# Keeping the last four V heads across the turn, with attention and layernorm in columns and wo read in long rows

## The chip, the cores and the metric

The kernel runs on one core of one Trainium2 chip. The time is the device time of the whole program in microseconds (us). Before the change its median is 1688.55 us over 3 runs, from 1687.66 to 1689.11. The core's engines are TensorE (PE, with its weight loads PEld), VectorE (DVE), ScalarE (ACT), GpSimd (POOL) and SyncE (SP). Each takes its instructions in its own order. SP issues the large transfers, which all go into one DMA queue; POOL issues a few small ones.

## What is computed

One decode step of a transformer block, and its backward pass. With B = 4 sequences, one query position, D = 512, H = 32 heads of Dh = 128, a cache of Sk = 4096 positions and F = 1792:

```
q  = layernorm(x) @ wq                        # B x H x Dh
p  = softmax(q . K / sqrt(Dh))                # per (b, h), over 4096 positions
O  = p . V                                    # per (b, h), 128 values
h  = x + concat(O) @ wo                       # B x 512
h2 = h + (silu(n @ w1) * (n @ w3)) @ w2       # n = layernorm(h)
```

The outputs are h2 and the gradients of x, of the K cache and the V cache (128 MiB each), of wq, wo, w1, w3 and w2, for a given gradient of h2. The caches are bf16; there are NH = 128 pairs (b, h), here called heads and numbered s, with b = s mod 4. The K or V of one head is 1 MiB. K and V are read once for the forward pass, V again for the backward pass (dP = dO . V), and dK and dV are written.

## The kernel before

**The arena.** Nearly all large data live in one on-chip arena of 23 slots of 8,320 bytes per partition; a slot holds the K or V of a head, a product, a page of wo, or half of w1 or w3 (`Slot`). `manual_schedule` keeps the program order as written: the order of the Python text is the order of each engine's queue, and a transfer is issued when its slot is free and SP has come to it.

**Forward.** Groups of two heads run through a loop. For each head s, K gives the scores and the softmax weights P; DVE multiplies K by P (`PK_mul`, L457, 2.29 us each); PE multiplies V by PK and P in 32 matmuls of 130 columns (`M_mm`, L472, 2.03 us), which gives a matrix M that the backward pass uses for dq, and in its last column the head's output O; `M_end` sums P*K (L482), and ACT copies M out (L486). `O_cols` (L502) picks the O column of 16 heads out of M. V's slot is given back after each head. Toward the end, `weights` also loads the four pages of wo (L586) and the four halves of w1 and w3 (L580).

**The middle.** After head 125's M comes a stretch that isn't a loop. `attn_page` (L517) multiplies O by one page of wo (8 heads) into rows of 512, interleaved with the products of heads 126 and 127; DVE adds the pages to x. Then layernorm of h in rows: transposes of h, statistics, the mean and inverse deviation spread to all partitions by a matmul, `hhatT` (L873). Then gate and up (`gu_ps`, L880, 56 matmuls of four columns each), with w1 and w3 transposed in place on PE between them (`pt_w`, L601; copied back by ACT and DVE, L254 and L256) because the backward pass needs them the other way. silu and its derivative follow on DVE, then `dn_ps` (L911), the gradient at the layernorm's output, with 112 matmuls. The layernorm backward gives `dhT` (L950). wo is also transposed in place, two heads at a time (`woT`, L610).

**Turn and backward.** `rep_ps` (L958) spreads dO of the first heads over all partitions; `grad_V` (outer product on DVE, L813; store L824) makes dV of head 0 and head 1. `dO_columns` gives dO for 32 heads. V of the first heads is loaded a second time (`load_V2`, L840), nine of them before the first store. Each V is transposed in four groups on PE and ACT (`V_T`, L798 and L799), then `front(s)` (through POOL's `zd`, L1211) computes dP for the softmax backward. Groups 0 and 1 of head 0 are transposed during the layernorm backward, groups 2 and 3 after `dO_columns`. `front(0)` stands ahead of the third `grad_V`. From there on the loop over heads, later over pairs (L1400), loads V, makes dV and dK and stores them, with weight gradients as side work.

The heads are worked in the order s = 0 to 127 in both passes.

Of the kernel before, what the change touches and what calls it, by code (L numbers as in the profile page):

```python
# [15 lines left out]
G = 2  # L16
# [7 lines left out]
OLD = 9  # L24


@with_exitstack
def kernel(
# [58 lines left out]
    def bh_of(s):  # L87
        return s % B, s // B

# [72 lines left out]
    rows_t = pers.tile([32 + B, D], FP32, name="rows_t")  # L162
    xr, xhat = rows_t[0:B, :], rows_t[32:32 + B, :]
    nc.gpsimd.dma_start(out=xr, in_=x2)
    gr_s = Slot("gr")
# [7 lines left out]
    Ks, Vs, KTs, PKs = {}, {}, {}, {}  # L173

    def load_K(s):
        if s < NH:
            Ks[s] = Slot("Kn")
            nc.sync.dma_start(out=Ks[s].heads(), in_=cache_head(A_k_cache, s))
# [3 lines left out]
    def load_V(s):  # L182
        if s < NH and s >= nvl["n"]:
            nvl["n"] = s + 1
            Vs[s] = Slot("Vn")
            nc.sync.dma_start(out=Vs[s].heads(), in_=cache_head(A_v_cache, s))
# [16 lines left out]
    sel_f = fcon.tile([P, H], FP32, name="sel_f")  # L203
# [37 lines left out]
    hrows = xr  # L241
    kPT = pers.tile([P, NH], FP32, name="kPT")
# [83 lines left out]

    def M_of(s):
# [38 lines left out]
    def q_stationaries(gi):  # L366
        W = fw.tile([P, G, 4, 32], BF16, name="W", tag="W", bufs=1)
        for hl in range(G):
            s = gi * G + hl
# [69 lines left out]
    def sm_P(gi):  # L439
# [5 lines left out]
        for q in range(4):  # L445
            r_ = slice(32 * q, 32 * (q + 1))
            nc.scalar.copy(out=P_all[r_, gi * G:(gi + 1) * G, :].rearrange("p g (c jj) -> p g c jj", c=4),  # L447
                           in_=v[r_, 0:G, :, :, q])

    def PK_pairs(s):  # L450
        PKs[s] = Slot("PK")
        PK = PKs[s].t[:].rearrange("p (j c) -> p j c", c=PKW)
        nc.gpsimd.tensor_copy(out=PK[:, :, Dh:PKW], in_=P_all[:, s, :, None].to_broadcast([P, SJ, 2]))  # L453
# [20 lines left out]
    def M_end(s):  # L474
# [13 lines left out]
        Vs.pop(s).give()  # L488

    def kP_flush(s):  # L490
        ks = Slot("kP_sb")
        kP_sb = ks.f(4 * Dh).rearrange("p (c d) -> p c d", c=4)
        nc.scalar.copy(out=kP_sb, in_=hold["kP"][:])
        kt_ps = psM.tile([P, PKW], FP32, tag="M", name="kt_ps")
        for c in range(4):
            nc.tensor.matmul(kt_ps[:, 0:H], lhsT=kP_sb[:, c, :], rhs=sel_f[:], start=(c == 0), stop=(c == 3))
        nc.scalar.copy(out=kPT[:, s - 31:s + 1], in_=kt_ps[:, 0:H])
# [3 lines left out]
    def O_cols(s0, s1):  # L501
        nc.vector.tensor_copy(out=OT_f[:, s0:s1], in_=Ms[s0 // MC].f(MC * (Dh + 1)).rearrange("p (n c) -> p n c", c=Dh + 1)[  # L502
            :, s0 % MC:s0 % MC + s1 - s0, Dh])
        nc.vector.tensor_copy(out=OT_bf[:, s0:s1], in_=OT_f[:, s0:s1])
# [5 lines left out]
    def attn_page(pg):  # L510
        last = pg == H // 8 - 1
        if pg == 0 or last:
            hold["at"] = psT.tile([P, 512], FP32, tag="tps", name="al_ps") if last else psX.tile([P, 512], FP32, tag="x", name="at_ps")
        at_ps = hold["at"]
        for k in range(8):
            c = 0 if last else k % 2
# [1030 lines left out]
```

## Time and profile before

| what | value |
|---|---|
| median of 3 runs | 1688.55 us |
| span of the profiled execution | 1686.6 us |
| PE, DVE, ACT, POOL busy | 75%, 73%, 57%, 23% of the span |
| bytes moved | 707.21 MB, mean 419 GB/s |
| share of the large queue | 99.2% |
| V heads loaded singly, loads of two heads | 160, 48 |
| one product M (32 matmuls) | 2.03 us |
| one PK_mul or grad_V on DVE | 2.29 us |
| gate's first matmul | at 678.49 us |
| first dV store issued | at 699.11 us |

The profiled execution's own time is its span of 1686.6 us; the timed runs are about 2 us longer, which includes what lies around the span. A row of a timeline gives the start, the duration, the engine, the line, the operation, output and inputs, the number of instructions, and in brackets the engine's idle time before it and what ended that. Rows of PE can overlap with rows of its weight loads. The DMA share is the mean over 16 DMA engines.

### The profile page before, as it was taken

The numbers are of one execution on the slowest core, as the hardware profiler recorded it, in microseconds if no ns is written. First come the engines' busy times: TensorE is split into PE (matmuls) and PEld (weight loads), VectorE is DVE, ScalarE is ACT, GpSimd is POOL, SyncE is SP. The second block draws the span as 40 slices with busy tenths as digits, with TensorE's granted clock in tenths as the row PEclk, the third lists the DMA queues.
The fourth block names the chain that finished last, engine by engine and source line by source line (L and its number), as shares of the span: only waits on it lengthen the run. The fifth ranks groups of instructions, "written<-read, shape, count | busy, mean of one in ns | idle before, by whom it ended". The sixth has DMA issues, their size and how long they took to land.

```text
span 1686.6 us, 33967 instructions
## 1 busy us (share of the span) xinstructions
PE 1260.6 (75%) x14188; PEld 924.3 (55%) x14188; DVE 1233.9 (73%) x1198; ACT 960.9 (57%) x1492; POOL 379.6 (23%) x663
## 2 busy tenths in 40 slices
PE   5989888888888888878878666667766677776660
PEld 4777777677667766745555544544434444444440
DVE  5999899989998997667766476576565656555673
ACT  3455454445445454677666556666655676666650
POOL 1221222222232222234541131111120101011020
PEclk9999999999999999799899778777678676567775
DMA  9999999999999999999999999999999999999996
GB/s 400 424 424 424 425 423 425 424 424 421 418 423 411 424 411 397 398 410 426 425 426 428 429 429 429 431 430 429 429 430 430 429 429 431 430 429 431 430 429 259
DMA packets 80986, 707.21 MB, mean 419 GB/s; under 512 B 8748, under 2 KB 12984, under 8 KB 15296
## 3 DMA queue, kind: packets, MB, share of 16 engines
q1 hardware_dynamic: 80416, 704.94, 99.2%
q8 instruction: 112, 1.84, 0.4%
q14 instruction: 42, 0.34, 0.0%
q0 software_dynamic: 416, 0.10, 0.0%
HBM read 422.59 MB, written 282.34 MB: 418 GB/s over the span
## 4 chain that ended last, share of the span: by engine, by line
DMA 35%; DVE 7%; ACT 5%; PE 5%; issue 3%; DVEq 0%; SPq 0%; POOL 0%; ACTq 0%
DMA out_dram<-arena 34%; DVE arena L1400 7%; ACT arena L799 5%; PE pt_tps L798 1%; PE dq_ps L1007 1%; PE dP_ps L1245 1%; DMA arena<-in_A_v_cache_dram 1%; PE pt_wo L610 0%; DVEq L1542 0%; PE rep_ps L1186 0%; DVE dPr L1342 0%; ACT dPr L1221 0%; PE dOT_ps L773 0%; PE dPT_ps L1228 0%; PE c_ps L784 0%
## 5 line engine op out<-in xcount | busy, mean ns | idle before, releaser
L799 ACT COPY arena<-pt_tps 128x1024 bf16<-128x1024 bf16 x512 | 491.7, 1023 | 249.0 <-PE pt_tps L798 247.3
L798 PE MATMUL pt_tps<-ident_f,arena 128*128 128x128 f32 x2048 | 410.7, 356 | 202.9 <-DMA arena<-in_A_v_cache_dram 125.6
L798 PEld LDWEIGHTS pt_tps<-ident_f,arena 128*128 128x128 f32 x2048 | 304.1, 182 | 349.3 <-issue 191.6
L1400 DVE TENSOR_TENSOR arena<-arena 128x8192 bf16<-128x8192 bf16 x48 | 212.5, 4427 | 197.9 <-DMA out_dram<-arena 192.5
L457 DVE TENSOR_TENSOR arena<-arena 128x4096 bf16<-128x4096 bf16 x128 | 292.4, 2285 | 24.0 <-POOL arena L453 24.0
L472 PE MATMUL M_ps<-arena 128*128 128x130 bf16 x4096 | 286.9, 223 | 30.0 <-DMA arena<-in_A_v_cache_dram 29.2
L472 PEld LDWEIGHTS <-arena 128*128 128x128 bf16 x4096 | 254.6, 99 | 49.6 <-DMA arena<-in_A_v_cache_dram 42.5
L1400 DVE TENSOR_TENSOR arena<-dS,arena 128x8192 bf16<-128x8192 bf16 x48 | 212.3, 4424 | 67.6 <-DMA out_dram<-arena 67.6
L364 DVE STREAM_TRANSPOSE arena<-arena 128x512 f32<-128x512 f32 (+1 forms) x321 | 250.6, 797 | 0.0
L359 ACT COPY arena<-pt_tps 128x1024 bf16<-128x1024 bf16 x128 | 129.4, 1012 | 180.4 <-PE pt_tps L358 149.6
L1397 POOL COPY arena<-arena 128x128 bf16<-128x128 bf16 x48 | 43.7, 912 | 432.7 <-ACT arena L1374 200.0
L370 POOL TENSOR_TENSOR W<-qrep,wmask 128x128 bf16<-128x128 bf16 x128 | 120.8, 944 | 85.4 <-PE S_ps L390 70.6
L453 POOL COPY arena<-P_all 128x64 bf16<-128x64 bf16 x128 | 32.7, 256 | 412.5 <-ACT P_all L447 409.5
L1308 POOL COPY arena<-arena 64x4 bf16<-64x4 bf16 x96 | 68.8, 717 | 136.3 <-PE dP_ps L1328 108.6
L1328 PE MATMUL dP_ps<-arena 128*32 128x512 bf16 x768 | 84.4, 471 | 8.4 <-ACT arena L799 8.3
L813 DVE TENSOR_TENSOR arena<-dS,arena 128x4096 bf16<-128x4096 bf16 x32 | 73.1, 2291 | 21.8 <-DMA out_dram<-arena 21.5
L447 ACT COPY P_all<-pt_P 32x64 bf16<-32x64 bf16 x256 | 52.1, 203 | 54.1 <-PE pt_P L443 51.8
L358 PE MATMUL pt_tps<-ident_b,arena 128*128 128x128 bf16 x1024 | 80.8, 224 | 0.0
L482 PE MATMUL kP_ps<-arena,onesw 128*32 128x512 bf16 x1024 | 79.4, 387 | 0.0
L813 DVE TENSOR_TENSOR arena<-P,arena 128x4096 bf16<-128x4096 bf16 x29 | 66.3, 2291 | 17.7 <-DMA out_dram<-arena 17.5
L422 ACT ACTIVATE E<-S_ps,nm 128x256 f32<-128x256 f32 x64 | 30.4, 474 | 82.7 <-DVE nm L419 82.6
L991 PE MATMUL gps<-arena 4*128 4x512 bf16 x110 | 47.3, 452 | 39.0 <-ACT arena L985 39.0
(246 smaller groups left out, 1494.7 us busy)
## 6 DMA issues: line engine op xcount, KB each, us to landing
out_dram<-arena SPq DMA_DIRECT2D x96, 2048.0 KB, 27.4
arena<-in_A_v_cache_dram SPq DMA_DIRECT2D x160, 1024.0 KB, 15.6
arena<-in_A_k_cache_dram SPq DMA_DIRECT2D x128, 1024.0 KB, 15.4
arena<-in_A_v_cache_dram SPq DMA_DIRECT2D x48, 2048.0 KB, 31.7
out_dram<-arena SPq DMA_DIRECT2D x72, 1024.0 KB, 19.8
arena<-in_A_wq_dram SPq DMA_DIRECT2D x8, 1024.0 KB, 14.3
arena<-in_B_w_dram SPq DMA_DIRECT2D x8, 896.0 KB, 15.0
out_dram<-arena SPq DMA_DIRECT2D x6, 896.0 KB, 27.6
```

The source lines that it names most:

```text
L358: nc.tensor.transpose(pt[:, i, :], Kn[:, c * GW + i, :], ident_b[:])
L359: nc.scalar.copy(out=KT[:, c * GW:(c + 1) * GW, :], in_=pt[:])
L364: nc.vector.transpose(out=KT[:, c * w_:(c + n) * w_], in_=Kn[:, c * w_:(c + n) * w_])
L370: nc.gpsimd.tensor_tensor(out=W[:, hl], in0=qrep[:, :, s:s + 1].to_broadcast([P, 4, 32]), in1=wmask[:, hl, None, :].to_broadcast([P, 4, 32 ...
L457: nc.vector.tensor_tensor(out=PK[:, :, 0:Dh].rearrange("p j (r t) -> p j r t", t=2), in0=Ks[s].heads().rearrange("p j (r t) -> p j r t", t=2),
L472: nc.tensor.matmul(hold["M"][:], lhsT=Vn[:, j, :], rhs=PK[:, j, :], start=(j == 0), stop=(j == SJ - 1))
L482: nc.tensor.matmul(hold["kP"][32 * q:32 * (q + 1), :, :], lhsT=ones_window(w), rhs=PK[:, j0:j0 + 4, 0:Dh], start=(w == 0 and c == 0), stop ...
L798: nc.tensor.transpose(ptw[:, jj, :], w[:, 4 * g + jj, :], ident_f[:])
L799: nc.scalar.copy(out=v.rearrange("p (j d) -> p j d", d=Dh)[:, g * GW:(g + 1) * GW, :], in_=pt[:])
L813: nc.vector.tensor_tensor(out=dst.rearrange("p j (r t) -> p j r t", t=2), in0=col2[:, :, None, :].to_broadcast([P, SJ, Dh // 2, 2]), in1=r ...
L1328: nc.tensor.matmul(rows["acc"][32 * c:32 * (c + 1), :], lhsT=zt[t % B][:, k, ZP - m:ZP - m + 32], rhs=words_of(v, 2 * c + u, k), start=(pl ...
L1400: nc.vector.tensor_tensor(out=dst.rearrange("p (j r t) -> p j r t", r=Dh // 2, t=2), in0=col2[:, :, None, :].to_broadcast([P, 2 * SJ, Dh / ...
```

## The change

It has these parts.

- **The heads' order.** Forward step f works on head col(f) = (f + 4) mod 128, so the last four steps are heads 0 to 3, the first of the backward pass. Their V slots aren't given back but kept (`kept`), and the second loading of V starts at head 4. Four V loads of 1 MiB fall away.
- **wo in rows of 4096 bytes.** A page's element order in the arena is now head, then partition p, then four consecutive rows 4p to 4p+3 of wo, instead of one row per partition. `O_mix` rearranges O to fit, with 16 small matmuls against every fourth column of the identity and a DVE copy (`Omix`).
- **Attention as columns.** `attn_x` puts x into the accumulator `at_ps` [128, 4, 4], from x loaded once more in columns by four small POOL transfers at the start (`xcols`). `attn_heads` then multiplies wo by O with four columns at a time: 16 matmuls for one step of four heads. `attn_page` goes.
- **The tail's order.** Before M_mm of head 126 stand `O_cols`, `O_mix` and `attn_heads(1, 2)`; the DVE copies of `O_cols` come behind `PK_mul(127)`. The last `O_cols`, `O_mix` and `attn_heads` come behind the last product.
- **Layernorm as columns.** Two matmuls against ones (`col_sums`) give the sums over partitions; `hc`, `sq`, `rb` and `hhatT` are built from `hT_f`. The rows of h and of the normalised h are made later, during the backward pass.
- **Transposes.** `woT_unit` now turns four heads (16 transposes, two copies). A slot `w1T` takes the first half of w1 transposed, so that the half itself is given back earlier. The w1 and w3 transposes are spread differently: one unit during the layernorm, four and one of wo between gate and up, the rest interleaved with `dn`. One wo unit takes the place of V of head 0 in the shadow of the layernorm backward, and all four groups of V of head 0 come after `dO_columns`.
- **silu.** What depends on the gate alone is done between gate and up.
- One constant of the later side work (`S0`) goes from 21 to 23.

```diff
+    def col(f):
+        return (f + KEEP) % NH
...
-    rows_t = pers.tile([32 + B, D], FP32, name="rows_t")
-    xr, xhat = rows_t[0:B, :], rows_t[32:32 + B, :]
+    rows_t = pers.tile([P, D], FP32, name="rows_t")
+    xr, xhat, hhat = (rows_t[i:i + B, :] for i in (0, 32, 96))
     nc.gpsimd.dma_start(out=xr, in_=x2)
+    xcols = rows_t[64:64 + DC * B, 0:P]
+    for c in range(DC):
+        nc.gpsimd.dma_start(out=xcols[c * B:(c + 1) * B, :], in_=x2[:, c * P:(c + 1) * P])
...
-        Vs.pop(s).give()
+        if s < NH - KEEP:
+            Vs.pop(s).give()
+        else:
+            kept[col(s)] = Vs.pop(s)
...
     def wo_page(h):
         return mid_w["wo"][h // 8].b(8 * D).rearrange("p (h c n) -> p h c n", h=8, c=DC)
 
 
-    def attn_page(pg):
-        last = pg == H // 8 - 1
-        if pg == 0 or last:
-            hold["at"] = psT.tile([P, 512], FP32, tag="tps", name="al_ps") if last else psX.tile([P, 512], FP32, tag="x", name="at_ps")
-        at_ps = hold["at"]
-        for k in range(8):
-            c = 0 if last else k % 2
-            nc.tensor.matmul(at_ps[32 * c:32 * c + B, :], lhsT=OT_bf[:, (8 * pg + k) * B:(8 * pg + k + 1) * B],
-                             rhs=wo_page(8 * pg)[:, k].rearrange("p c n -> p (c n)"),
-                             start=(k == 0 if last else pg == 0 and k < 2), stop=(k == 7 if last else pg == H // 8 - 2 and k >= 6),
-                             tile_position=(0, 32 * c))
-        if pg >= H // 8 - 2:
-            for c in range(1 if last else 2):
-                nc.vector.tensor_tensor(out=hrows, in0=hrows, in1=at_ps[32 * c:32 * c + B, :], op=ALU.add)
+    def attn_x():
+        hold["at"] = psX.tile([P, DC, B], FP32, tag="x", name="at_ps")
+        r_ = slice(64, 64 + DC * B)
+        nc.tensor.matmul(hold["at"].rearrange("p c b -> p (c b)"), lhsT=xcols, rhs=ident_f[r_, r_], start=True, stop=False)
+
+    def O_mix(c0, c1):
+        ps = psT.tile([P, 4, H // 4, B], FP32, tag="tps", name="mix_ps")
+        ov = OT_bf.rearrange("p (c i b) -> p i c b", i=4, b=B)
+        for k in range(4):
+            for i in range(4):
+                nc.tensor.matmul(ps[32 * i:32 * (i + 1), k, c0:c1, :], lhsT=ident_b[:, k:P:4], rhs=ov[:, i, c0:c1, :],
+                                 start=True, stop=True, tile_position=(0, 32 * i))
+        nc.vector.tensor_copy(out=Omix[:, :, c0:c1, :], in_=ps[:, :, c0:c1, :])
+
+    def attn_heads(c0, c1, last=False):
+        for c in range(c0, c1):
+            wn = mid_w["wo"][c // 2].b(8 * D).rearrange("p (c k j) -> p c k j", c=2, k=4)[:, c % 2]
+            for k in range(4):
+                for jj in range(DC):
+                    nc.tensor.matmul(hold["at"][:, jj, :], lhsT=wn[:, k, jj * P:(jj + 1) * P], rhs=Omix[:, k, c, :],
+                                     start=False, stop=last and c == c1 - 1 and k == 3 and jj == DC - 1)
...
-        nc.sync.dma_start(out=sl.b(8 * D).rearrange("p (h j) -> p h j", h=8),
-                          in_=A_wo[pg * 8 * P:(pg + 1) * 8 * P, :].rearrange("(h p) j -> p h j", p=P))
+        nc.sync.dma_start(out=sl.b(8 * D).rearrange("p (c n) -> p c n", c=2),
+                          in_=A_wo[pg * 8 * P:(pg + 1) * 8 * P, :].rearrange("(c p k) j -> p c (k j)", c=2, k=4))
...
-    def woT_unit(ps, u, eng):
-        v = wo_page(2 * u)[:, 2 * u % 8:2 * u % 8 + 2]
-        pt = ps.tile([P, 2, DC, P], BF16, tag="tps", name="pt_wo")
-        for i in range(2):
-            for c in range(DC):
-                nc.tensor.transpose(pt[:, i, c, :], v[:, i, c, :], ident_b[:])
-        evac_copy(v, pt[:], eng)
+    def woT_unit(ps, u, engs):
+        wn = mid_w["wo"][u // 2].b(8 * D).rearrange("p (c k j) -> p c k j", c=2, k=4)[:, u % 2]
+        wt = wo_page(4 * u)[:, 4 * u % 8:4 * u % 8 + 4].rearrange("p i jj (m k) -> p jj i m k", k=4)
+        pts = []
+        for z in range(2):
+            pts.append(ps.tile([P, 2, 4, P], BF16, tag="tps", name="pt_wo"))
+            for jj in range(2):
+                for k in range(4):
+                    nc.tensor.transpose(pts[z][:, jj, k, :], wn[:, k, (2 * z + jj) * P:(2 * z + jj + 1) * P], ident_b[:])
+        for z in range(2):
+            evac_copy(wt[:, 2 * z:2 * z + 2], pts[z].rearrange("p jj k (i m) -> p jj i m k", i=4), engs[z])
...
     weights(NGI)
     PK_pairs(NH - 1)
...
     M_end(NH - 3)
     PK_mul(NH - 1)
     weights(NGI)
-    attn_page(0)
+    O_cols(NH - MC, NH - KEEP)
+    attn_x()
+    O_mix(1, 8)
+    attn_heads(1, 2)
     M_mm(NH - 2, 0, SJ)
     M_end(NH - 2)
     weights(NGI)
-    attn_page(1)
-    woT(2, "sv")
+    attn_heads(2, 4)
     M_mm(NH - 1, 0, SJ)
     M_end(NH - 1)
     weights(NGI)
-    O_cols(NH - MC, NH)
-    attn_page(2)
-    attn_page(3)
-    kP_flush(NH - 1)
-    weights(NGI)
+    O_cols(NH - KEEP, NH)
+    O_mix(0, 1)
+    attn_heads(4, 6)
+    attn_heads(0, 1)
+    attn_heads(6, 8, True)
     assert not pending
+    nc.vector.tensor_copy(out=hT_f[:], in_=hold["at"][:])
+    ks_last = kP_copy()
...
-    V2s, VTs = {}, {}
+    V2s, VTs = dict(kept), {}
...
-    nv = {"next": 0}
+    nv = {"next": KEEP}
...
+        w1T = Slot("w1T")
+        mid_t.update(w1=[w1T, mid_w["w1"][1]], w3=mid_w["w3"])
...
+        def col_sums(src, name):
+            ps = psA.tile([P, DC, B], FP32, tag="rT", name="cs_ps")
+            nc.tensor.matmul(ps.rearrange("p c b -> p (c b)"), lhsT=ones_f[:], rhs=src.rearrange("p c b -> p (c b)"),
+                             start=True, stop=True)
+            s_ = mid.tile([P, B], FP32, name=name)
+            nc.vector.tensor_reduce(out=s_[:], in_=ps.rearrange("p c b -> p b c"), axis=AX.X, op=ALU.add)
+            return s_
+
+        hc = mid.tile([P, DC, B], FP32, name="hc")
+        sq = mid.tile([P, DC, B], FP32, name="sq")
+        hsum = col_sums(hT_f, "hsum")
+        nc.vector.scalar_tensor_tensor(out=hc[:], in0=hsum[:, None, :].to_broadcast([P, DC, B]), scalar=-1.0 / D,
+                                       in1=hT_f[:], op0=ALU.mult, op1=ALU.add)
+        nc.vector.tensor_tensor(out=sq[:], in0=hc[:], in1=hc[:], op=ALU.mult)
+        w13T(1, "s")
+        rb = col_sums(sq, "rb")
+        nc.vector.tensor_scalar(out=rb[:], in0=rb[:], scalar1=1.0 / D, scalar2=eps, op0=ALU.mult, op1=ALU.add)
+        nc.scalar.sqrt(rb[:], rb[:])
         nc.scalar.activation(out=warm[:], in_=warm[:], func=AF.Exp)
-        woT(2, "s")
-        rdiag = mid.tile([B, 2 * B], FP32, name="rdiag")
-        nc.vector.tensor_scalar(out=rdiag[:, 0:B], in0=ident_f[0:B, 0:B], scalar1=mv[:, 0:1], scalar2=None, op0=ALU.mult)
-        nc.vector.reciprocal(out=rstd_h[:], in_=rstd_h[:])
-        nc.vector.tensor_scalar(out=rdiag[:, B:2 * B], in0=ident_f[0:B, 0:B], scalar1=rstd_h[:], scalar2=None, op0=ALU.mult)
-        rb_ps = psA.tile([P, 2 * B], FP32, tag="rT", name="rb_ps")
-        nc.tensor.matmul(rb_ps[:], lhsT=ones_f[0:B, :], rhs=rdiag[:], start=True, stop=True)
-        rb = mid.tile([P, 2 * B], FP32, name="rb")
-        nc.vector.tensor_copy(out=rb[:], in_=rb_ps[:])
+        kP_flush(NH - 1, ks_last, psA.tile([P, PKW], FP32, tag="rT", name="kt_ps"))
+        nc.vector.reciprocal(out=rb[:], in_=rb[:])
         hhatT = mid.tile([P, DC, B], BF16, name="hhatT")
-        hhatT_f = mid.tile([P, DC, B], FP32, name="hhatT_f")
-        nc.vector.tensor_tensor(out=hhatT_f[:], in0=pt[:], in1=rb[:, None, 0:B].to_broadcast([P, DC, B]), op=ALU.subtract)
-        nc.vector.tensor_tensor(out=hhatT[:], in0=hhatT_f[:], in1=rb[:, None, B:2 * B].to_broadcast([P, DC, B]), op=ALU.mult)
-        nc.vector.tensor_tensor(out=hhatT_f[:], in0=hhatT_f[:], in1=rb[:, None, B:2 * B].to_broadcast([P, DC, B]), op=ALU.mult)
+        nc.vector.tensor_tensor(out=hhatT[:], in0=hc[:], in1=rb[:, None, :].to_broadcast([P, DC, B]), op=ALU.mult)
+        nc.vector.tensor_tensor(out=hhatT_f[:], in0=hc[:], in1=rb[:, None, :].to_broadcast([P, DC, B]), op=ALU.mult)
...
-                w13T(4, "sv")
-        gateT = mid.tile([P, FC, B], FP32, name="gateT")
-        sigT = mid.tile([P, FC, B], FP32, name="sigT")
-        siluT = mid.tile([P, FC, B], FP32, name="siluT")
-        t1 = mid.tile([P, FC, B], FP32, name="t1")
-        t2 = mid.tile([P, FC, B], FP32, name="t2")
-
-        nc.scalar.activation(out=sigT[:], in_=gu_ps[:, 0], func=AF.Exp, scale=-1.0)
+                nc.scalar.activation(out=sigT[:], in_=gu_ps[:, 0], func=AF.Exp, scale=-1.0)
+                w13T(2, "ss")
+                nc.vector.tensor_copy(out=gateT[:], in_=gu_ps[:, 0])
+                nc.vector.tensor_scalar(out=sigT[:], in0=sigT[:], scalar1=1.0, scalar2=None, op0=ALU.add)
+                nc.vector.reciprocal(out=sigT[:], in_=sigT[:])
+                nc.vector.tensor_tensor(out=siluT[:], in0=gateT[:], in1=sigT[:], op=ALU.mult)
+                nc.vector.tensor_tensor(out=d_upT_bf[:], in0=d_hhT[:], in1=siluT[:], op=ALU.mult)
+                nc.vector.tensor_tensor(out=t1[:], in0=gateT[:], in1=siluT[:], op=ALU.subtract)
+                nc.vector.scalar_tensor_tensor(out=t1[:], in0=t1[:], scalar=1.0, in1=sigT[:], op0=ALU.add, op1=ALU.mult)
+                woT(1, "sv")
+                w13T(2, "vs")
+                w1[0].give()
+                while free:
+                    load_V2()
...
-        w13T(len(tunits), "sssvsvsvsvvs")
 
         dn_ps = psC.tile([P, DC, B], FP32, tag="dn", name="dn_ps")
-        for jj in range(DC):
-            i_mm = 0
-            for (lt, wt) in ((d_gateT_bf, w1), (d_upT_bf, w3)):
-                for fc in range(FC):
-                    nc.tensor.matmul(dn_ps[:, jj, :], lhsT=w13_view(wt, jj)[:, fc * P:(fc + 1) * P], rhs=lt[:, fc, :],
-                                     start=(i_mm == 0), stop=(i_mm == 2 * FC - 1))
-                    i_mm += 1
-        for sl in w1 + w3:
+        n_dn = {"n": 0}
+        nc.tensor.matmul(dn_ps.rearrange("p c b -> p (c b)"), lhsT=ident_b[:], rhs=zeros[:], start=True, stop=False)
+
+        def dn_unit(nm, i, k):
+            lt = d_gateT_bf if nm == "w1" else d_upT_bf
+            for jj in (2 * i, 2 * i + 1):
+                for fc in range(k, min(k + 4, FC)):
+                    nc.tensor.matmul(dn_ps[:, jj, :], lhsT=w13_view(mid_t[nm], jj)[:, fc * P:(fc + 1) * P], rhs=lt[:, fc, :],
+                                     start=False, stop=n_dn["n"] == 2 * DC * FC - 1)
+                    n_dn["n"] += 1
+
+        engs = deque("svsvsvvsvsv")
+        while turned:
+            if tunits:
+                w13T(1, engs.popleft())
+            if len(tunits) < 9:
+                for _ in range(2 if tunits else len(turned)):
+                    if len(turned) > (2 if tunits else 0):
+                        dn_unit(*turned.popleft())
...
-        V_T(0, psT, range(2))
+        woT(1, "ss")
...
-        V_T(0, psT, range(2, SJ // GW))
+        V_T(0, psT)
```

## The prediction

> **What bounds the kernel now.** I read the busy shares and slices first, then the queue, then windows of 5 us around the middle, then each engine's timeline there.
>
> ```profile
> span 1686.6 us, 33967 instructions
> DMA  9999999999999999999999999999999999999996
> DMA packets 80986, 707.21 MB, mean 419 GB/s; under 512 B 8748, under 2 KB 12984, under 8 KB 15296
> ```
>
> The queue is busy in every slice but the last: as a whole the kernel is bound by bytes, and a V head of 1 MiB lasts 2.46 us in it (1,048,576 B at the 425 GB/s of most slices). So four V loads fewer look like 9.8 us. But a byte is worth its time only where the queue decides. The columns of the next view are the window, then busy us and instructions of PE, PE's weight loads, DVE, ACT and POOL, then the granted TensorE clock, the DMA share and GB/s.
>
> ```profile
> 655.00:660.00 5.00, 3.56 (x51) 2.92 (x52) 2.50 (x7) 1.53 (x4) 0.53 (x1) 1.00 1.04 372
> 660.00:665.00 5.00, 4.92 (x76) 3.51 (x75) 3.37 (x2) 3.06 (x9) 0.24 (x1) 1.00 1.04 320
> 675.00:680.00 5.00, 4.05 (x88) 3.82 (x88) 2.72 (x11) 3.50 (x6) 0.00 (x0) 1.00 1.04 422
> 680.00:685.00 5.00, 5.00 (x100) 5.00 (x97) 1.98 (x6) 2.85 (x6) 0.00 (x0) 0.58 1.01 423
> 700.00:705.00 5.00, 2.80 (x21) 1.66 (x21) 3.00 (x3) 1.81 (x4) 4.67 (x15) 0.63 1.00 405
> 705.00:710.00 5.00, 4.18 (x22) 2.36 (x21) 3.87 (x3) 3.85 (x4) 1.49 (x3) 0.69 0.70 293
> ```
>
> Two places matter: the queue is slow (320 to 372 GB/s) while wo comes in rows of 1024 bytes, and it runs dry (0.70) in 705 to 710. The timelines say why it does.
>
> ```profile
> 665.37 2.03 PE L472 MATMUL M_ps<-arena 128*128 128x130 bf16 x32
> 665.56 2.29 DVE L457 TENSOR_TENSOR arena<-arena 128x4096 bf16<-128x4096 bf16 x1 [0.34 <-POOL arena L453]
> 667.78 1.03 PE L517 MATMUL at_ps<-arena,OT_bf 128*4 128x512 bf16 x8
> 668.74 1.07 PE L610 MATMUL pt_wo<-ident_b,arena 128*128 128x128 bf16 x16
> 669.64 2.04 PE L472 MATMUL M_ps<-arena 128*128 128x130 bf16 x32
> ...
> 678.49 1.54 PE L880 MATMUL gu_ps<-hhatT,arena 128*128 128x4 bf16 x56 [0.68 <-DVE hhatT L873]
> 679.89 2.35 PE L601 MATMUL pt_w<-ident_b,arena 128*128 128x128 bf16 x28
> 683.64 7.04 PE L601 MATMUL pt_w<-ident_b,arena 128*128 128x128 bf16 x84
> ```
> ```profile
> 669.51 24.92 SPq L840 DMA_DIRECT2D arena<-in_A_v_cache_dram  x9
> 699.11 17.89 SPq L824 DMA_DIRECT2D out_dram<-arena  x7
> ```
> ```profile
> 695.08 1.93 ACT L799 COPY arena<-pt_tps 128x1024 bf16<-128x1024 bf16 x2 [0.69 <-PE pt_tps L798]
> 698.95 1.93 ACT L799 COPY arena<-pt_tps 128x1024 bf16<-128x1024 bf16 x2 [0.77 <-PE pt_tps L798]
> ```
> ```profile
> 703.71 2.31 DVE L813 TENSOR_TENSOR arena<-arena 128x4096 bf16<-128x4096 bf16 x1 [2.00 <-POOL zd L1211]
> ```
>
> The last nine V loads have landed by 701.33, and the first store (dV of head 0) is issued at 699.11, out of a chain that is PE and DVE from 665 on: last M products, gate, transposes of w1/w3, dn, layernorm backward, dO. The third store comes at 706.04, after front(0), and that is the hole. In both kernels nine V heads stand in the arena before the first store, and after it both move the same bytes. So the four loads come out of a stretch in which compute sets the end, and the question is when the stores start.
>
> **The parts.** Times of one profiled execution; its 1686.6 lies 1.95 under the median of 1688.55, and I add differences to the median.
>
> Tail of the forward pass. PE's new order has O_mix between kP(125) and M_mm(126). O_mix needs O_cols(112..123), queued on DVE behind PK_mul(127): 665.56 + 2.29 = 667.85, then two copies of 0.18 and 0.17, 668.25 with the hand-over. Before, M_mm(126) began at 665.37. Behind 668.25 come 16 small matmuls (0.44 at 56 in 1.54, L880; 1.07 if like the 16 of L610; 0.5 taken, nearest to L880 by width), the Omix copy on DVE (0.25, between DVE copies of 0.17 and 0.29), 16 N=4 matmuls 0.44, M_mm(126) with kP 2.41 (665.37 to 667.78), 32 matmuls 0.88, M_mm(127) 2.03, with hand-overs 0.15: end near 674.9, where before had 671.67 with two pages of 1.03 and 1.07 of transposes inside. Behind the waiting O_mix on PE stand M_mm(126) and M_mm(127), and ACT's copies of M and the last columns of O wait for those. **+3.2.**
>
> M(127) to gate. Before 678.49 - 671.67 = 6.82. After: ACT copy 0.3, O_cols 0.4, O_mix 0.5, copy 0.25, 80 N=4 matmuls 2.2, hT copy 0.2, two column sums at 0.6 with their reduce, four DVE steps of 0.18 to 0.2, the root behind an ACT evacuation of 1.0: 6.35. **-0.5.** Bounds: -1.5 if the evacuation is done in time, +0.5 if hand-overs are as long as the 0.68 before the gate.
>
> Gate to dn's end. Before 693.47 - 678.49 = 14.98, nearly all PE. After, the same gate, up and dn, 8 transposes moved out ahead, 16 of wo moved in: 8 x 0.084 (7.04/84) = +0.7, less 0.3 because silu's DVE steps come earlier. **+0.4** (0 to +1.3). The weights are there: wo's pages at 2.46 instead of 3.2 us and no load is behind them that the gate waits for.
>
> dn's end to the first store: 699.11 - 693.47 = 5.64 in both. First store near 702.3.
>
> V of head 0. Before, two of its four evacuation pairs lie in the shadow of layernorm backward (695.08 to 697.01). After, woT(1) stands there and all four follow dO: **+1.9** (two at 0.97), less 0.35 since POOL's zd has one copy less before it (+1.0 to +2.3). It stands ahead of dP, zd and the third grad_V, so that store lags 3.1 + 1.6 = 4.7.
>
> The hole. Before loses 1.5 us (0.30 of 5) in 705 to 710. After, loads are done well before the first store, so the queue is dry longer; but the lag is counted at the third store, and 0.6 of the old loss follows it and isn't lost twice (stores come each 2.3, a store lasts 2.46). **-0.6** (-1.5 to 0).
>
> Start. Four more POOL issues, each 0.55 (that of the gradient rows at 1.92), put the identity 2.2 later. DVE waits for x until 7.45 and wq lands at 13.5: **0**; with the cover gone, +2.2. SP issues four V loads less, and the rows of h and hhat, built later from columns (8 transposes and two ACT copies), lie beside stores that never let the queue run dry: 0.
>
> Clock. PE would stand idle from about 664.5 to 668.3. The one row of it here is 680 to 685, a clock of 0.58 with PE busy 5.00, after 56 matmuls of four columns. Transposes there cost 0.084 against 0.067 (1.07/16) at full clock. After has more such N=4 stretches: 0 to 2.4, **+0.4**. The Trainium skill ("TensorE: Matmul & The Clock Gate", "HAM oscillation — how this bites in real kernels") says that a PE idle gap over about 3.4 us halves the clock. The trace agrees only partly: its clock falls without idle time. By that rule both last M products would run at half clock, which would add the price of the first rival below: 1696 instead of 1693.
>
> Sum: 3.2 - 0.5 + 0.4 + 1.6 - 0.6 + 0.4 = **+4.5, 1693.0.** From the hole on the queue is never dry, so a late store stays late to the end.
>
> **Rivals.**
> Half clock on the tail (0.20). The gap of 3.8 us would be PE's longest in this stretch, and at 680 the clock fell with PE busy. M_mm(126), M_mm(127) at 2.03 each and their kP would then run partly at 0.58, some 2.5 to 3 more than the sum: 1696. Against it: full clock stands in every window from 655 to 680.
>
> No change (0.27). O_mix waits 1.5 less than I say, because the last two products on DVE come earlier than before; the column layernorm saves its full 1.5 (1.0 more) and the clock costs nothing: 4.5 - 1.5 - 1.0 - 0.4 = +1.6, about 1690. For it speaks only that several of my terms are small hand-overs.
>
> Faster (0.15). The queue, not compute, sets the first stores: the hole at 705 is only a bubble, and a store issued at 699.11 that is done at 704.04 has waited behind loads done at 701.33. Then four loads (9.8) and 3 us of wo come off: 1676 to 1679. It decides only if the queue still has a backlog when the first store is issued; before it was 701.33 - 699.11 = 2.2, so at most about 2 us come of it unless compute also gets earlier. For it: nothing but the full slices.
>
> **How the numbers follow.** Main case 0.38, own range 1690.5 to 1697 (the bounds above added in quadrature, about 3 each way). A measurement tells 0.2%, 3.4 us, from no change, so slower means above 1691.9. Slower: 0.38 + 0.20 = 0.58; same 0.27; faster 0.15. The range reaches down into the faster case's weaker half, a gain of 3, and up past half clock: 1685.5 to 1698.5; outside it lie 0.13 below and 0.06 above.
>
> **What would show it.** PE idle before O_mix from 664.5 to 668; M(127) ending near 675; gate near 681; first store near 702, third near 710.5; a DMA share far under 1 from about 680 to the first store; windows of wo at 420 GB/s; four ACT evacuations in a row ahead of the third store. I am wrong if M(127) ends by 672, if the first store is issued before 699, or if the share stays near 1 up to it.

## The result, and the profile after

The changed kernel takes 1704.18 us (median of 4 runs, 1703.07 to 1705.51) against 1688.82 before: a ratio of 1.0092, with a 95% interval from 1.0078 to 1.0107. It is slower by 15.4 us. The forecast had 4.5, within a range that ended at 1698.5.

The head of the page after; the second line has the DMA share and the third GB/s, each in 40 slices of the span:

```profile
span 1703.7 us, 34245 instructions
DMA  9999999999999999599999999999999999999995
GB/s 397 418 419 418 419 419 419 419 419 416 417 414 410 418 404 412 216 405 426 426 426 428 427 427 428 429 429 430 429 429 430 429 430 430 431 429 430 428 428 250
DMA packets 77467, 703.04 MB, mean 413 GB/s; under 512 B 8796, under 2 KB 8952, under 8 KB 12288
```

The same third line of the kernel before:

```profile
GB/s 400 424 424 424 425 423 425 424 424 421 418 423 411 424 411 397 398 410 426 425 426 428 429 429 429 431 430 429 429 430 430 429 429 431 430 429 431 430 429 259
```

Two things are to be seen. The four loads did go: 703.04 MB instead of 707.21. The middle has a hole, 216 GB/s in slice 17, as forecast. But slices 2 to 9, in the forward pass, run at 418 to 419 GB/s instead of 423 to 425, and nothing in the forecast speaks of that.

DVE and PE of the changed kernel from the last `PK_mul` to the gate, two timelines:

```profile
672.56 2.29 DVE L469 TENSOR_TENSOR arena<-arena 128x4096 bf16<-128x4096 bf16 x1 [0.33 <-POOL zeros L919]
```
```profile
668.98 2.04 PE L484 MATMUL M_ps<-arena 128*128 128x130 bf16 x32
675.20 0.32 PE L539 MATMUL mix_ps<-OT_bf,ident_b 128*32 128x28 bf16 x15 [3.17 <-DVE OT_bf L523]
676.38 3.63 PE L484 MATMUL M_ps<-arena 128*128 128x130 bf16 x32
681.79 3.63 PE L484 MATMUL M_ps<-arena 128*128 128x130 bf16 x32
692.34 1.66 PE L929 MATMUL gu_ps<-hhatT,arena 128*128 128x4 bf16 x56
```

The last `PK_mul` starts 7.0 us later than before (665.56). Then PE waits 3.17 us for the columns of O (the forecast had 3.8 us of idle time there), and both last products take 3.63 us instead of 2.03. Windows of the changed kernel; columns as in the prediction (busy us of PE, PEld, DVE, ACT, POOL; granted clock; DMA share; GB/s):

```profile
670.00:675.00 5.00, 2.02 (x29) 1.36 (x27) 4.63 (x4) 0.27 (x1) 0.28 (x2) 1.00 1.02 406
675.00:680.00 5.00, 4.36 (x67) 4.16 (x70) 0.42 (x2) 0.00 (x0) 0.00 (x0) 0.50 1.03 404
680.00:685.00 5.00, 5.00 (x72) 4.17 (x72) 0.00 (x0) 0.27 (x1) 0.58 (x3) 0.50 0.66 260
690.00:695.00 5.00, 5.00 (x82) 4.90 (x80) 1.54 (x9) 3.02 (x8) 0.00 (x0) 0.50 0.31 87
```

The granted clock is 1.00 while PE waits and 0.50 in the ten us behind (from 675.04 to 685.28 by the trace's clock record). The Trainium skill ("TensorE: Matmul & The Clock Gate", "HAM oscillation — how this bites in real kernels") says that PE idle gaps over about 3.4 us bring the throttled clock; here a wait of 3.17 us, with nothing but small matmuls beside it from 671.50 to 676.38, was followed by it. The queue's share falls under 1 from 680 on: the loads of the weights are done, the next load of V isn't issued before 686.01 because it waits 11.1 us for the sums of P*K behind the late last product, and no store is ready.

Where the 15 us to the first store come from, all from starts and ends in the two profiled executions:

| stretch | before | after | difference |
|---|---|---|---|
| start to the last PK_mul | 665.56 | 672.56 | +7.0 |
| to the end of the last product | 6.12 | 12.86 | +6.7 |
| to the gate | 6.81 | 6.92 | +0.1 |
| gate to dn's end | 14.98 | 16.26 | +1.3 |
| dn's end to the first store | 5.64 | 5.47 | -0.2 |
| first store issued | 699.11 | 714.07 | +15.0 |

The store queue of SP after:

```profile
686.01 20.97 SPq L872 DMA_DIRECT2D arena<-in_A_v_cache_dram  x5
714.07 17.25 SPq L856 DMA_DIRECT2D out_dram<-arena  x7
```

So there were two questions: why the forward pass is slower though it moves the same bytes, and whether the tail's 6.7 us are the wait and the clock.

### The profile page after: what moved, and what is told of

It is laid out like the page before. It is cut to its first block, busy times and chain, and to the rows that moved or that the text cites. A ratio compares the mean times of both kernels' runs of the same rounds, so it can differ in the third digit from the quotient of the medians.

```text
span 1703.7 us, 34245 instructions
## 1 busy us (share of the span) xinstructions
PE 1261.6 (74%) x14325; PEld 927.6 (54%) x14325; DVE 1232.0 (72%) x1198; ACT 960.4 (56%) x1495; POOL 378.7 (22%) x668
## 2 busy tenths in 40 slices
DMA packets 77467, 703.04 MB, mean 413 GB/s; under 512 B 8796, under 2 KB 8952, under 8 KB 12288
## 4 chain that ended last, share of the span: by engine, by line
DMA 35%; DVE 7%; ACT 6%; PE 5%; issue 2%; POOL 1%; DVEq 0%; SPq 0%; ACTq 0%; POOLq 0%
DMA out_dram<-arena 33%; DVE arena L1462 7%; ACT arena L831 6%; DMA arena<-in_A_v_cache_dram 2%; PE pt_tps L830 2%; PE dP_ps L1307 1%; PE dq_ps L1067 1%; POOL zd L1273 1%; ACT arena L263 0%; PE pt_wo L636 0%; DVEq L1604 0%; PE rep_ps L1248 0%; DVE dPr L1404 0%; POOL P L1278 0%; PE dPT_ps L1290 0%
## 5 line engine op out<-in xcount | busy, mean ns | idle before, releaser
L484 PEld LDWEIGHTS <-arena 128*128 128x128 bf16 x4096 | 255.2, 100 | 80.7 <-DMA arena<-in_A_v_cache_dram 75.8
L370 PEld LDWEIGHTS <-arena 128*128 128x128 bf16 x1024 | 62.1, 100 | 25.9 <-issue 25.8
```

The costliest lines, as they stand in the source:

```text
L370: nc.tensor.transpose(pt[:, i, :], Kn[:, c * GW + i, :], ident_b[:])
L484: nc.tensor.matmul(hold["M"][:], lhsT=Vn[:, j, :], rhs=PK[:, j, :], start=(j == 0), stop=(j == SJ - 1))
```

## The experiments

### The small loads at the start, and the tail's order

The trace's own records of the packets in the large queue show the slow forward pass more closely. The table counts packets of 8192 bytes that started between 20 and 640 us, and, in the right column, the share at 310 ns or less between 760 and 1500 us, when stores run too. It also holds the runs that follow:

```
run                                   share taking 310 ns or less   median    760-1500
before                                          0.94                309 ns      0.96
after                                           0.15                312 ns      0.94
x from rows (after, no small loads)             0.16                312 ns      0.94
before with the small loads                     0.95                309 ns      0.96
after, arena 64 bytes on                        0.94                309 ns      0.96
before, arena 64 bytes on                       0.14                312 ns      0.93
before, arena 32 bytes on                       0.14                313 ns      0.94
```

The first theory (A) was that the four small POOL loads at the start upset the queue. One kernel takes them away, another adds them to the kernel before:

```diff
-    xcols = rows_t[64:64 + DC * B, 0:P]
-    for c in range(DC):
-        nc.gpsimd.dma_start(out=xcols[c * B:(c + 1) * B, :], in_=x2[:, c * P:(c + 1) * P])
...
+        for c in range(DC):
+            nc.tensor.matmul(hold["at"][:, c, :], lhsT=xr[:, c * P:(c + 1) * P], rhs=ident_f[0:B, 0:B], start=(c == 0), stop=False)
```

> The changed kernel without its four extra small loads on POOL at the start: x in columns is made on PE from the rows of x that are there anyway. In the profile of the changed kernel the forward pass is 7.0 us late already at the last PK_mul (672.56 against 665.56), and a packet of 8192 bytes takes 312 to 319 ns in most cases where before it took 309. Theory A (the four small loads at the start put the DMA engines out of step, and they stay so through the forward pass): packets back at 309 ns, last PK_mul near 665.6, time near 1697. Rival B (the other order of the heads, that is the addresses read, makes the packets slower): nothing changes, last PK_mul near 672.5, time near 1704.

Measured: 1703.63 (1.0089, interval 1.0074 to 1.0104), the last `PK_mul` at 673.41, packets at 312 ns. Nothing changed.

> The kernel before, with the four small loads of x in columns added on POOL at the start and nothing else; what they load is not used. Theory A: the forward pass runs at 312 ns a packet, the last PK_mul starts near 672.5 and the time is near 1695.5. Rival B: no change, 1688.8. By my prediction's term for the start (hidden, 0, or 2.2 with the cover gone) it would be 1688.8 to 1691.

Measured: 1688.94 (1.0004, 0.9995 to 1.0014), the last `PK_mul` at 665.63. Theory A falls in both directions: the four loads cost nothing that shows.

The third kernel changes PE's order in the tail, the fourth has both edits:

```diff
     O_cols(NH - MC, NH - KEEP)
-    attn_x()
-    O_mix(1, 8)
-    attn_heads(1, 2)
     M_mm(NH - 2, 0, SJ)
     M_end(NH - 2)
     weights(NGI)
-    attn_heads(2, 4)
+    attn_x()
     M_mm(NH - 1, 0, SJ)
+    O_mix(1, 8)
     M_end(NH - 1)
     weights(NGI)
     O_cols(NH - KEEP, NH)
+    attn_heads(1, 5)
     O_mix(0, 1)
-    attn_heads(4, 6)
+    attn_heads(5, 7)
     attn_heads(0, 1)
-    attn_heads(6, 8, True)
+    attn_heads(7, 8, True)
```

> The changed kernel with the products of heads 126 and 127 put straight behind each other on PE; O_mix stands behind the second, and all of attention behind that. In the profile of the changed kernel PE waits 3.17 us for O_cols, both products then run at half clock (3.63 us instead of 2.03), and from the last PK_mul (672.56) to the end of the last product it takes 12.86 us, against 6.1 before. If that wait and the clock that falls in it are the cause: products back at 2.03 us, the gate 5.5 to 7 us earlier, time 1697 to 1699. Rival: the clock falls anyway because of the many matmuls of four columns, or the queue sets the stores: less than 3 us gained, 1701 to 1704.

> Both edits together: x in columns made on PE and the tail's order without the wait. If the two causes are separate and both on the path, the gains add: 1704.2 - 7 - 6.5 = 1690.5, with the first store near 700.5 instead of 714.07. If one of them only hides the other, it is no better than the better of the two alone, near 1697.

Measured: 1700.30 and 1700.15 (both 1.0070, 1.0055 to 1.0085). The tail's order gives 3.9 us, between the two expectations. In the third kernel's trace both products are back at 2.03 and 2.05 us, and `hT_f`, the end of attention, comes 9.1 us after the last `PK_mul` starts instead of 16.05: 7 us in that execution, though its last `PK_mul` itself comes 1.1 us later (673.65). Two more kernels have the changed kernel's order in the tail: the one with x from rows and the one with the arena moved (below). Their PE timelines, in this order:

```profile
676.05 0.33 PE L536 MATMUL mix_ps<-OT_bf,ident_b 128*32 128x28 bf16 x15 [2.52 <-DVE OT_bf L520]
677.23 3.63 PE L481 MATMUL M_ps<-arena 128*128 128x130 bf16 x32
682.59 2.03 PE L481 MATMUL M_ps<-arena 128*128 128x130 bf16 x32
```
```profile
668.09 0.32 PE L539 MATMUL mix_ps<-OT_bf,ident_b 128*32 128x28 bf16 x15 [3.17 <-DVE OT_bf L523]
669.27 3.63 PE L484 MATMUL M_ps<-arena 128*128 128x130 bf16 x32
674.64 2.04 PE L484 MATMUL M_ps<-arena 128*128 128x130 bf16 x32
```

In both, only the first product takes 3.63 us. So a wait ahead of the products is there each time, one of 2.52 us was followed by half clock too, and how much the clock adds differs between executions; that can hide part of what the new order gains. The new order takes away the wait and the small matmuls beside it together, so which of the two brings the half clock stays open.

### Where the arena begins

The remaining theories were the order of the heads (B: other addresses are read) and something that moved in on-chip memory (C). In the compiled programs the arena begins at byte 30336 of each partition before and 30528 after, because small tiles ahead of it changed. 30336 is 237 x 128; 30528 is 238.5 x 128. A slot has 8320 bytes, 65 x 128, so what holds for the first slot holds for all. Each kernel has one tile made larger, and nothing else (the few small tiles behind it move by the same bytes):

```diff
-    hT_f = pers.tile([P, DC, B], FP32, name="hT_f")
+    hT_f = pers.tile([P, 2 * DC, B], FP32, name="hT_f")[:, 0:DC]
```
```diff
-    kPT = pers.tile([P, NH], FP32, name="kPT")
+    kPT = pers.tile([P, NH + 16], FP32, name="kPT")[:, 0:NH]
```

> The changed kernel with hT_f given twice its size and nothing else, so that everything allocated after it, the arena too, lies 64 bytes further on: the arena begins at byte 30592 of a partition instead of 30528 (before the change: 30336). 30336 and 30592 are multiples of 128, 30528 is one of 64 only. Theory C (where the arena begins makes its incoming packets slower, 312 ns instead of 309): packets back at 309 ns, the last PK_mul near 665.6 instead of 672.6, time 7 us less, near 1697. Theory B (the other order of the heads, that is the addresses read, makes them slower): no change, 1704.

> The kernel before with one small tile 64 bytes larger and nothing else, so that the arena begins at byte 30400, a multiple of 64 but not of 128. Theory C: packets at 312 ns in the forward pass, the last PK_mul 7 us later, time near 1695.5. Theory B: no change, 1688.

Measured: the changed kernel with the arena at 30592 takes 1694.22 (1.0040, 1.0026 to 1.0053), 10.0 us less, though its five runs lie from 1692.83 to 1698.21; the kernel before with the arena at 30400 takes 1697.93 (1.0054, 1.0039 to 1.0069), 9.2 us more. The last `PK_mul` of the two, in this order, from their DVE timelines:

```profile
665.45 2.29 DVE L469 TENSOR_TENSOR arena<-arena 128x4096 bf16<-128x4096 bf16 x1 [0.33 <-POOL zeros L919]
```
```profile
672.38 2.29 DVE L457 TENSOR_TENSOR arena<-arena 128x4096 bf16<-128x4096 bf16 x1 [0.34 <-POOL arena L453]
```

Each kernel now has the other's time there. Theory C holds and B falls: the second kernel reads the heads in the old order and is slow, the first in the new order and is fast. DVE's products last 2.29 in both, so it is the loads and not the engines that are slower.

At the last `PK_mul` the shift is 7 us; the rest comes later. In the six profiled executions with the arena off a multiple of 128, the time from the start of the third `grad_V` to the end of the span is 984.0 to 985.0 us; in the eight with it on one, 982.1 to 984.3.

A finer offset, again in the kernel before (`NH + 8`, so that the arena begins at 30368):

> The kernel before with the arena at byte 30368, a multiple of 32 but not of 64. With the arena at 30400 (64 off a multiple of 128) it took 1697.9 and packets in the forward pass took 312 ns instead of 309. If what counts is only whether a packet of 8192 bytes begins on a multiple of 128: as slow as at 30400, near 1698. If it gets worse with finer offsets: slower than that, 1705 or more. If only the one position at 64 is bad: 1688.7.

Measured: 1698.26 (1.0056, 1.0041 to 1.0072): as slow as 64 bytes off, no slower. The two starts on a multiple of 128 are fast, and 32 and 64 off are alike. The Trainium skill ("DMA: Bandwidth & Descriptors", "How a descriptor splits into AXI transactions") says that a descriptor that doesn't start on a multiple of 256 bytes fetches unused bytes ahead of its start, which cost extra beats. What these runs move is the address that is written, and there 256 is not the boundary: slots of 8320 bytes stand at 0 and 128 off a multiple of 256 by turns, and 0.94 of all packets take 309 ns.

### The tail's order with the arena in place, and the four loads

> The changed kernel with both edits: the arena 64 bytes further on, and the products of heads 126 and 127 straight behind each other on PE with attention behind them. The tail's order alone gave 3.9 us (1704.2 to 1700.3). Theory C: 1700.3 - 7 = 1693. Theory B: 1700.

Measured: 1689.55 (1.0007, 0.9997 to 1.0016), 4.7 us under the run with the arena alone. Its PE timeline:

```profile
665.33 2.03 PE L484 MATMUL M_ps<-arena 128*128 128x130 bf16 x32 [0.81 <-DVE arena L469]
668.17 2.04 PE L484 MATMUL M_ps<-arena 128*128 128x130 bf16 x32
670.14 0.31 PE L539 MATMUL mix_ps<-OT_bf,ident_b 128*32 128x28 bf16 x16
670.90 1.75 PE L548 MATMUL at_ps<-Omix,arena 128*128 128x4 bf16 x64
```

With two edits, one of placement and one of order, 14.6 of the 15.4 us are gone, though the kernel loads and computes what the changed kernel does. What is left cannot be told from no change.

The next kernel takes away what the change is named for. V of heads 0 to 3 is given back and loaded again:

```diff
-        if s < NH - KEEP:
-            Vs.pop(s).give()
-        else:
-            kept[col(s)] = Vs.pop(s)
+        Vs.pop(s).give()
...
-    nv = {"next": KEEP}
+    nv = {"next": 0}
```

> The run before this one (arena 64 bytes further on, tail's order), but V of heads 0 to 3 is given back after the forward pass and loaded a second time, so four loads of 1 MiB more. My prediction's reading (the four loads come out of a stretch in which compute sets the end): within 1.5 us of the run before this one. Rival (the queue sets when the stores start): 4 x 2.46 = 9.8 us more.

Measured: 1690.19 (1.0007, 0.9998 to 1.0017), 0.6 us more than the run before it, which is not clear of noise. First the queue of SP with V kept, then with V reloaded:

```profile
670.95 20.91 SPq L871 DMA_DIRECT2D arena<-in_A_v_cache_dram  x5
698.95 17.16 SPq L855 DMA_DIRECT2D out_dram<-arena  x7
```
```profile
667.61 24.83 SPq L868 DMA_DIRECT2D arena<-in_A_v_cache_dram  x9
699.51 17.60 SPq L852 DMA_DIRECT2D out_dram<-arena  x7
```

Nine loads instead of five, and the first store is issued 0.56 us later. The windows show where the four went. With V kept, then with V reloaded:

```profile
675.00:680.00 5.00, 4.62 (x65) 4.62 (x65) 1.31 (x8) 2.76 (x6) 0.00 (x0) 0.50 0.62 248
685.00:690.00 5.00, 5.00 (x146) 5.00 (x144) 2.78 (x7) 3.33 (x5) 0.00 (x0) 1.00 0.54 198
```
```profile
675.00:680.00 5.00, 4.62 (x75) 4.60 (x75) 1.31 (x8) 2.83 (x6) 0.00 (x0) 0.50 1.02 419
685.00:690.00 5.00, 4.42 (x122) 4.35 (x120) 2.72 (x7) 3.18 (x5) 0.00 (x0) 1.00 1.00 419
```

PE's busy time is nearly the same; the queue is full in one and half empty in the other. The 4 MiB lay beside compute.

### The long rows of wo alone

The kernel before, with the long rows and without the mixing of O that goes with them:

```diff
-        nc.sync.dma_start(out=sl.b(8 * D).rearrange("p (h j) -> p h j", h=8),
-                          in_=A_wo[pg * 8 * P:(pg + 1) * 8 * P, :].rearrange("(h p) j -> p h j", p=P))
+        nc.sync.dma_start(out=sl.b(8 * D).rearrange("p (c n) -> p c n", c=2),
+                          in_=A_wo[pg * 8 * P:(pg + 1) * 8 * P, :].rearrange("(c p k) j -> p c (k j)", c=2, k=4))
```

> The kernel before, with wo read in rows of 4096 bytes and nothing else; O isn't mixed to fit, so the attention output is a sum over the wrong rows of wo (it leaves that part of the computation undone). It measures what the long rows alone are worth: the four pages should land in 2.46 us each instead of 3.2, so the queue is 3 us ahead from there on. My prediction's reading: nothing waits for that, 0 to 1 us less, 1688 to 1689. Rival: the queue's 3 us come off, 1685.7.

Measured: 1688.20 (0.9997, 0.9988 to 1.0006). The window that had 320 GB/s, and the hole:

```profile
660.00:665.00 5.00, 4.92 (x77) 3.55 (x76) 3.37 (x2) 3.10 (x9) 0.24 (x1) 1.00 1.02 411
705.00:710.00 5.00, 4.07 (x22) 2.43 (x20) 5.00 (x3) 3.85 (x4) 4.88 (x3) 0.71 0.69 283
```

The long rows do what they promise (411 instead of 320), and the time does not move.

### Two attempts to shorten the middle

If compute from the last product to the first store sets the time, shortening it should pay. The first attempt starts from the kernel with both edits (1689.55):

```diff
-        w13T(1, "s")
+        first = woT_steps(psT, wo_units.popleft())
+        next(first)
         rb = col_sums(sq, "rb")
+        next(first)
...
-        kP_flush(NH - 1, ks_last, psA.tile([P, PKW], FP32, tag="rT", name="kt_ps"))
+        for _ in first:
+            pass
...
-                w13T(2, "vs")
+                w13T(3, "vsv")
...
+        kP_flush(NH - 1, ks_last, psA.tile([P, PKW], FP32, tag="rT", name="kt_ps"))
...
-        woT(1, "ss")
+        V_T(0, psT, range(2))
...
-        V_T(0, psT)
+        V_T(0, psT, range(2, SJ // GW))
```

Here `woT_steps` is `woT_unit` in three steps: eight transposes, eight more, then both copies on ACT.

> An attempt at a version that beats both: the arena 64 bytes further on, the tail's order (the run with both took 1689.55), and in the middle: the first unit of wo is transposed in the layernorm in place of a unit of w1, with its ACT copies behind the root; the last kP sum (1.9 us of PE ahead of the gate) goes behind up; and the first half of V of head 0 goes back into the shadow of the layernorm backward, where woT stood. By my prediction's reading (compute in the middle sets when the stores start): gate about 1.3 us earlier, the third store 2 to 2.6 us earlier, 1687 to 1688. Rival (PE's transposes only move within the same 15 us between gate and dn, the queue's hole stays): 1689.5.

Measured: 1690.04 (1.0009, 1.0000 to 1.0018). The gate came 0.75 us earlier (678.05 instead of 678.80), but dn ended 1.4 later, because the transposes and the kP sum now stand between gate and dn. The third `grad_V` began 6.92 us after the first instead of 7.45: half of V of head 0 in the shadow is worth 0.5, not the 1.6 that I had priced.

The second attempt only changes places in the layernorm:

```diff
-        w13T(1, "s")
+        kP_flush(NH - 1, ks_last, psA.tile([P, PKW], FP32, tag="rT", name="kt_ps"))
         rb = col_sums(sq, "rb")
...
-        kP_flush(NH - 1, ks_last, psA.tile([P, PKW], FP32, tag="rT", name="kt_ps"))
+        w13T(1, "s")
```

> The run with the arena 64 bytes further on and the tail's order (1689.55, ratio to before 1.0007), with two things changed places in the layernorm: the last kP sum goes ahead of the second column sum, into PE's wait for it, and the unit of w1 goes behind the root, so that the root no longer stands behind ACT's copy of 1.01 us and the gate no longer behind 1.9 us of kP sums. By the reading that compute in the middle sets when the stores start: gate near 677.8 instead of 678.80, first store and time about 1 us less, 1688.5. Rival (what the gate gains is lost again by dn, because the transposes at half clock fill the time): 1689.5.

Measured: 1689.86 (1.0009, 1.0000 to 1.0018). The gate came at 677.73, as expected, and the first store at 699.03, no earlier than 698.95. The gain was lost on PE in dn, in the first of these lines:

```profile
689.38 0.34 PE L960 MATMUL dn_ps<-d_gateT_bf,arena 128*128 128x4 bf16 x8 [1.12 <-issue]
693.11 0.45 PE L960 MATMUL dn_ps<-d_upT_bf,arena 128*128 128x4 bf16 x12 [0.42 <-ACT arena L263]
```

"issue" is idle time in which PE waited for nothing that the profile shows. The kernel it started from has no such wait in dn; the changed kernel has one of 0.55 us. What causes it was not tried, but the traces point to PE's own instructions: the small queue that the profile calls "instruction" (q8) carries one packet of 16384 bytes for every 256 instructions of PE (112 for 28615 instruction records before, 113 for 28888 after), and each of the eleven such waits of 0.2 us or more in the fourteen traces ends 1.3 to 1.7 us after the end of such a packet, here 1.49. That is not shown by a run. No version was found that beats the kernel before.

## Why the prediction was right or wrong

The direction was right and the size was not: 15.4 us instead of 4.5, outside the range. The step that failed first is not one of the six terms of the sum but the term for the start, put at 0, and with it the ground under the tail. The tail was worked out from before's own start of the last `PK_mul`, "665.56 + 2.29 = 667.85", as if the forward pass up to there took the same. It took 7.0 us longer, because the arena moved by 192 bytes to a start that is no multiple of 128; on the whole time that is worth 9 to 10 us, shown in both directions. My section on the start looked at POOL's four loads, which cost nothing that shows, and not at where the tiles went. The second failing step is the tail's clock, below.

Without that shift the changed kernel takes 1694.22 against 1688.71, +5.5 where the sum had +4.5. That they lie so near is in part luck: in its profiled execution, 5.0 us over before's, the terms are +5.1, -0.1, +0.1, -0.2, +0.9 and -0.8, so a tail priced too low is partly made up for by terms priced too high. Term by term:

- **Tail, +3.2.** The mechanism was right: O_mix behind O_cols behind the last `PK_mul`, PE idle, both products queued behind it. Measured +6.7 in the profiled execution (12.86 instead of 6.12), and +5.1 in the run with the arena moved. O's columns came 2.64 us after the last `PK_mul` began, where 2.69 was forecast, and PE waited 3.17 us of the 3.8. What was mis-sized is the clock: 3.63 instead of 2.03 for one product or both. That was the first rival, to which I gave 0.20 and +2.5 to 3; two products at 1.60 more make 3.2, with kP at 1.04 instead of 0.62 beside it. Against it I had set that the clock was full from 655 to 680 before; but there PE's longest wait was 1.15 us. The row that I went by, a fall at 680 with PE busy, shows another way to half clock than this one.
- **Last product to gate, -0.5.** Measured +0.1 (6.92 against 6.81). The column layernorm saves nothing that shows. The terms that I listed there, with two column sums at 0.6, in fact add up to 6.8 and not to 6.35, so they gave 0.
- **Gate to dn, +0.4.** Measured +1.3, the end of the bounds, with the clock at 0.50 in 690 to 695 and 0.55 of "issue" in dn; +0.1 in the run with the arena moved (15.08).
- **dn to the first store, 0.** Measured -0.2.
- **V of head 0, +1.6.** Mis-sized: the third store's lag grew by 0.6 over the first's (721.57 - 706.04 = 15.5 against 15.0), and by 0.9 in the run with the arena moved. The four copies do stand in a row on ACT, but before, too, the third `grad_V` waited 2.00 us for POOL's zd, so ACT was only part of the way.
- **The hole, -0.6, and the clock, +0.4.** No run measures them alone. Between the third store (+15.5) and the end of the span (+17.1 in this execution) 1.6 were lost, but the arena's start lies in that too: in the run with the arena moved, 0.8 were gained (+5.8 to +5.0), near the forecast and no more than single executions differ by. What the clock added lies mostly in the tail.

The reading under the whole sum held: the four loads and the long rows are worth 0.6 and 0.4 us by the medians, neither clear of noise, where the queue's own price for them would be 9.8 and 3. The rival "faster" thus falls, and for the reason given against it, that compute sets the first stores. The figure beside that reason was off: the last V load before the first store didn't land by 701.33; its 16 parts landed from 700.25 to 704.43, so the backlog at 699.11 was up to 5.3 us and not 2.2. That the tail costs nothing ("no change") falls too, as the change stands; with the tail's order and the arena's start put right, it is what remains.

## What to carry to other kernels

Before counting instructions, ask what a change does to where the large buffers begin: adding or widening a small tile ahead of one big buffer moved every large load off a multiple of 128 bytes and cost more than everything that the change meant to do. Bytes saved pay only where the queue is the last thing waited for; a stretch with a full queue may still be set by compute, and running it with the bytes put back tells which. When an instruction is placed ahead of PE's dense work, price its wait and then price the work behind it at half clock.

## What the runs showed of the hardware that I had not expected

Packets of 8192 bytes into on-chip addresses that are 32 or 64 bytes off a multiple of 128 take 312 to 313 ns in the median instead of 309, and the forward pass, which only loads, falls from 424 to 419 GB/s. Not every transfer pays: with the same arena, the first loads of the program (6 to 12 us) took 309 ns for 0.92 of their packets, and so did the packets of the stretch with loads and stores from 760 us on (0.93 to 0.94, with 0.96 where the arena starts on a multiple of 128). What about the forward loads makes them sensitive, the work of the engines beside them, their number under way, or the lack of stores, was not tried and stays open; so does what makes the rest of the program 1 to 2 us longer.

What the clock takes after a wait isn't fixed: of two kernels with the same tail and the same wait of 3.17 us, one had both products at 3.63 us in its profile, the other the first at 3.63 and the second at 2.04. In the clock records of all fourteen traces the clock is 1.0 or 0.5, and each stretch at 0.5 that ends inside the program is a whole multiple of 3.413 us long: here 10.24 us in the first kernel and 6.83 in the second, whose second product began 0.5 us after the clock was back.
